# Seven products of half tiles in place of eight, in the output product of groups two to six

## The chip, the cores and the metric

The kernel runs on one NeuronCore of a Trainium2 chip. The metric is the device time of one execution in microseconds; where several runs were timed, their median.

## The reference

A gated linear attention runs over 4 batches, 8 heads, 768 steps and head size 48; its output, put together over the heads, goes through a feed-forward layer with a squared ReLU.

```python
for t in range(S):
    state = alpha[:, :, t, :, None] * state + np.einsum('bhd,bhe->bhde', k[:, :, t], v[:, :, t])
    y[:, :, t] = np.einsum('bhd,bhde->bhe', q[:, :, t], state)
...
x = np.ascontiguousarray(attn_out.transpose(0, 2, 1, 3)).reshape(B * S, H * D)
...
h = np.maximum(x @ w_in, 0.0)
return (h * h @ w_out).astype(np.float32)
```

x is 3072 x 384, w_in 384 x 2048, w_out 2048 x 384. The weights come as float64, everything else as float32.

## The kernel before, in words

The sequence is cut into chunks of 128 steps. One chunk of one batch is a block, so there are 24 blocks, four (the four batches of one chunk) to a group, and six groups. Each block goes through four stages of attention (line 402). Stage 1: aT turns alpha on TensorE, ln takes logarithms on ScalarE, sn sums them along the chunk on VectorE, eb and ei make the exponentials on ScalarE. Stage 2: qT and kT turn q and k, mq and mk scale them on VectorE into qs and ks. Stage 3: sc multiplies ks and qs, am masks the result on VectorE, kr turns ks back and kc copies it. Stage 4: kv makes the state's increment, sm and st update the state on VectorE, y makes the output, and ev copies it on ScalarE, in 12 pieces a block, into xT, the transposed input of the feed-forward layer.

The feed-forward layer works on a whole group of 512 rows. ffn_in (line 365) makes one of 16 hidden tiles of 128 x 512: three matmul calls of 512 columns, a ReLU on ScalarE into r, a square into hid, in group one on ScalarE and later on VectorE. ffn_out (line 381) is the output product: for each of four blocks t of the group, 16 calls of 384 columns are summed in one PSUM bank, 64 calls a group. ScalarE copies the bank out, and SP stores it. The weights stay in on-chip memory from group one on; there they are converted from float64, one of 16 pieces a slot (convert_first, convert_second).

The order is written out by hand: every engine works through its own queue in the program's order. The first blocks follow a list of steps (line 407). After that each group has 16 slots, one for each stage of each block of the next group (line 420). A slot emits its stage, one piece of weights, in the first slot of a block the loads of the block after, and then as many units of this group's feed-forward layer as its share of the columns allows. So the first eight slots hold two ffn_in units each, and the last eight hold four ffn_out units each. The last group has no attention beside it.

Buffers: three input tiles each for alpha, q and k, and four for v (NIN and NV, line 74); two of most work tiles (line 204); 16 hidden tiles; four PSUM banks for the feed-forward layer (ps_ffn) and four for attention. All loads and stores go through the queue of SP, in order, and a load waits there until its tile has been read.

Of the kernel before, what the change touches and what calls it, by code (L numbers as in the profile page):

```python
# [8 lines left out]
FP32 = mybir.dt.float32  # L9
U32 = mybir.dt.uint32  # L10
AF = mybir.ActivationFunctionType
ALU = mybir.AluOpType
# [3 lines left out]
GB = 4  # L16
# [7 lines left out]
def kernel(  # L24
# [22 lines left out]
    nc = tc.nc  # L47
    B, H, S, D = q.shape
    C = 128
    NCH = S // C  # L50
    NP = H // 2
    NBLK = B * NCH
    DM, DF = moe_w_in.shape
    KM = DM // 128
    NJ = DF // 128
# [4 lines left out]
    consts = ctx.enter_context(tc.tile_pool(name="consts", bufs=1))  # L60
    raw_pool = ctx.enter_context(tc.tile_pool(name="raw", bufs=NR))
    cv_pool = ctx.enter_context(tc.tile_pool(name="cv", bufs=2))
    hid_pool = ctx.enter_context(tc.tile_pool(name="hid", bufs=NJ))
    p2 = ctx.enter_context(tc.tile_pool(name="p2", bufs=2))
    x_pool = ctx.enter_context(tc.tile_pool(name="x", bufs=2))
    ps_att = ctx.enter_context(tc.tile_pool(name="ps_att", bufs=4, space=PSUM))
    ps_ffn = ctx.enter_context(tc.tile_pool(name="ps_ffn", bufs=GB, space=PSUM))
# [3 lines left out]
    def kept(name, n, shape):  # L71
        return [consts.tile(shape, FP32, name=f"{name}{i}") for i in range(n)]

    NIN = 3
    NV = 4
    tiles = {x: kept(f"{x}_in", NIN, [128, H, 64]) for x in "aqk"}
    for i in range(NIN):
        for x, value in (("a", 1.0), ("q", 0.0), ("k", 0.0)):
            nc.gpsimd.memset(tiles[x][i][:, :, D:64], value)
    tiles["v"] = kept("v_in", NV, [128, H * D])  # L80
    s_t = kept("s", B, [128, NP, 128])
# [6 lines left out]
    def load(n, xs="aqkv"):  # L88
        c, b = divmod(n, B)
        for x in xs:  # L90
            t = tiles[x][n % len(tiles[x])]
            nc.sync.dma_start(
                out=t.rearrange("a (h d) -> a h d", h=H) if x == "v" else t[:, :, 0:D],
                in_=srcs[x][b, :, c * C : (c + 1) * C, :].rearrange("h s d -> s h d"),
            )

    NW = 8
    w_in = [consts.tile([128, KM, DF // NW], FP32, name=f"w_in{i}") for i in range(NW)]
    w_out = [consts.tile([128, NJ // NW, DM], FP32, name=f"w_out{i}") for i in range(NW)]
    raws = {}  # L100

    def load_weights(i):
        dst = (w_in + w_out)[i]
        dt = moe_w_in.dtype
        raw = dst if dt == FP32 else raw_pool.tile(list(dst.shape), dt, tag="raw", name="raw")
        raws[i] = raw
        if i < NW:
            src = moe_w_in[:, i * DF // NW : (i + 1) * DF // NW]
            nc.sync.dma_start(out=raw, in_=src.rearrange("(k r) f -> r k f", r=128))
        else:  # L110
            i -= NW
            src = moe_w_out[i * DF // NW : (i + 1) * DF // NW, :]
            nc.sync.dma_start(out=raw, in_=src.rearrange("(j r) m -> r j m", r=128))
# [29 lines left out]
    def convert_second(i):  # L143
        if moe_w_in.dtype == FP32:
            return
        w, hi, power, upper = half.pop(i)
        nc.vector.scalar_tensor_tensor(  # L147
            out=power, in0=hi, scalar=0x80000000, in1=power,
            op0=ALU.bitwise_and, op1=ALU.bitwise_or,
        )  # L150
        nc.vector.scalar_tensor_tensor(
            out=w, in0=upper, scalar=2.0**-20, in1=w, op0=ALU.mult, op1=ALU.add
        )
        nc.vector.tensor_tensor(out=w, in0=w, in1=power.bitcast(FP32), op=ALU.mult)  # L154

    for n, xs in ((0, "aqk"), (1, "aqk"), (2, "a"), (0, "v"), (2, "qk")):
        load(n, xs)
    to_load = list(range(2 * NW))
    stage = [2]
# [1 line left out]
    def next_weights():  # L161
        i = stage[0]
        stage[0] += 1
        if to_load:
            load_weights(to_load.pop(0))
        if i <= 2 * NW:
            convert_second(i - 1)
        if i < 2 * NW:
            convert_first(i)
# [18 lines left out]
    for _ in range(2):  # L188
        nc.tensor.matmul(
            out=ps_att.tile([128, NP, C], FP32, tag="att", name="warm"),  # L190
            lhsT=am_t[0][:, 0, 0, :], rhs=am_t[0][:, 0], start=True, stop=True,
# [3 lines left out]
    blk = [{} for _ in range(NBLK)]  # L195
# [5 lines left out]
            return ps_ffn.tile([128, *shape], FP32, tag="f", name=name)  # L201
        return ps_att.tile([128, *shape], FP32, tag="att", name=name)

    def work(name, bufs=2):
        return p2.tile([128, NP, C], FP32, tag=name, name=name, bufs=bufs)

    def turned(x, n):
        rows = tiles[x][n % NIN].rearrange("a h d -> a (h d)")
        ps = blk[n][f"{x}T"] = bank(n, f"{x}T")
# [70 lines left out]

    def kc(n):
        if n // B < NCH - 1:
            t = blk[n]["kc"] = work("kc")
            nc.scalar.activation(out=t, in_=blk[n].pop("kr"), func=AF.Copy)  # L284

    def kv(n):
        if n // B < NCH - 1:
            ps = blk[n]["kv"] = bank(n, "kv", (NP, 2 * D))
            for p in range(NP):
                nc.tensor.matmul(  # L290
                    out=ps[:, p, :], lhsT=blk[n]["kc"][:, p, :],
                    rhs=tiles["v"][n % NV][:, 2 * p * D : 2 * (p + 1) * D], start=True, stop=True,
                )
# [4 lines left out]

    def sm(n):
        if n // B in range(1, NCH - 1):  # L300
            ps, t = blk[n]["kv"], p2.tile([128, NP, 2 * D], FP32, tag="sm", name="sm")
            for e in range(2):
                rows, s = state(n, e)
                cols = slice(e * D, (e + 1) * D)
                nc.vector.tensor_tensor(  # L305
                    out=t[rows, :, cols], in0=ps[rows, :, cols], in1=s, op=ALU.add
                )
            blk[n]["kv"] = t

    def y(n):  # L310
        v_in = tiles["v"][n % NV]

# [47 lines left out]
        blk[n].clear()  # L360


    hid, acc = {}, {}

    def ffn_in(g, j):
        hid[j] = hid_pool.tile([128, GB * C], FP32, tag="hid", name="hid")
        w, c0 = w_in[j * NW // NJ], j % (NJ // NW) * 128
        ps = ps_ffn.tile([128, GB * C], FP32, tag="f", name="h")
        for kk in range(KM):
            nc.tensor.matmul(  # L370
                out=ps, lhsT=w[:, kk, c0 : c0 + 128], rhs=xT[g][:, kk, :],
                start=(kk == 0), stop=(kk == KM - 1),
            )
        r = p2.tile([128, GB * C], FP32, tag="r", name="r")
        nc.scalar.activation(out=r, in_=ps, func=AF.Relu)  # L375
        if g == 0:
            nc.scalar.activation(out=hid[j], in_=r, func=AF.Square)  # L377
        else:
            nc.vector.tensor_tensor(out=hid[j], in0=r, in1=r, op=ALU.mult)  # L379

    def ffn_out(g, t, i):
        per = NJ // NW
        if i == 0:
            acc[t] = ps_ffn.tile([128, GB * C], FP32, tag="f", name="o")
        for j in range(per * i, per * (i + 1)):
            nc.tensor.matmul(  # L386
                out=acc[t][:, 0:DM],
                lhsT=hid[j][:, t * C : (t + 1) * C],
                rhs=w_out[i][:, j % per, :],
                start=(j == 0), stop=(j == NJ - 1),  # L390
            )
        if i == NW - 1:
            o = p2.tile([128, DM], FP32, tag="osb", name="osb")
            nc.scalar.activation(out=o, in_=acc.pop(t)[:, 0:DM], func=AF.Copy)  # L394
            c, b = divmod(g * GB + t, B)
            r0 = (b * NCH + c) * C
            nc.sync.dma_start(out=out[r0 : r0 + C, :], in_=o)

# [4 lines left out]
    steps["weights"] = lambda: load_weights(to_load.pop(0))  # L405
    steps["first"], steps["second"] = convert_first, convert_second
    first = """
        aT0 ln0 sn0 qT0 eb0 kT0 ei0 mq0 mk0 aT1 kr0 ln1 sc0 load3a load1v load3q load3k load2v
        weights load3v weights sn1 kc0 qT1 am0 eb1 kT1 ei1 mk1 load4a weights load4q load4k weights
        aT2 mq1 kr1 ln2 sc1 kc1 sn2 y0 am1 ei2 kv0 eb2 ev0 qT2 st0 kT2 load4v mq2 aT3 mk2 kr2 ln3  # L410
        sc2 kc2 sn3 kv1 am2 ei3 y1 eb3 kT3 ev1 st1 qT3 mk3 y2 mq3 sc3 ev2 kv2 am3 kr3 first0 y3
        st2 kc3 ev3 second0 kv3 first1 st3
    """
    for word in first.split():
        f = next(x for x in steps if word.startswith(x))
# [2 lines left out]

    NS = GB * len(stages)
    for g in range(NBLK // GB):  # L420
        units = [(ffn_in, (g, j)) for j in range(NJ)]

        outs = [(g, t, i) for t in range(GB) for i in range(NW)]
        units += [(ffn_out, a) for a in (outs if g else sorted(outs, key=lambda a: a[2]))]
        cost = {ffn_in: KM * GB * C, ffn_out: NJ // NW * DM}
        total = sum(cost[f] for f, _ in units)
        done = 0
        for slot in range(NS):
            i, s = divmod(slot, len(stages))
            n = (g + 1) * GB + i  # L430
            if n < NBLK:
                for f in stages[s]:
                    f(n)
            next_weights()
            if s == 0 and n + 1 < NBLK:
                load(n + 1)
            while units and done * NS < total * (slot + 1):
                f, args = units.pop(0)
                f(*args)
                done += cost[f]  # L440
# [30 lines left out]
```

## Time and profile before

| | |
|---|---|
| three runs | 654.16, 656.03 and 657.51 us, median 656.03 |
| the profiled execution | 653.49 us |
| its span, first to last instruction | 651.5 us |
| granted TensorE clock, mean | 0.994 |
| busy: TensorE, weight loads, VectorE, ScalarE | 638.5, 375.4, 233.3, 230.1 us |
| DMA | 36.63 MB, 56 GB/s over the span |

Engines are named as in the profile: PE is TensorE and PEld its weight loads, DVE is VectorE, ACT is ScalarE, SP issues the DMAs. A row of the costliest groups gives line, engine, operation, output and inputs, shape and count; then busy time in us and the mean of one in ns; then the idle time of the engine ahead of them and what ended it. Matmul records overlap, since each counts its own drain, so a mean is longer than the distance between two of them. The chain of waits is followed back from the last instruction to whatever released each step.

### The profile page before, as it was taken

To read this page: it belongs to the slowest core of one execution; us is meant where nothing else is said; L and a number is where in the kernel's file an instruction comes from. 1 tells how busy PE (TensorE), PEld (TensorE's weight loads), DVE (VectorE), ACT (ScalarE), POOL (GpSimd) and SP (SyncE) were. 2 spreads that over 40 slices of the span, in tenths; PEclk is the share of its full clock that TensorE was granted. 3 is DMA by queue.
4 is the path that set the end of the run, shared out by engine and by line. 5 is a ranking of instruction groups with operands and counts; after the bars stand their busy time and mean duration, and the time that the engine had idled before them with its cause. 6 is when DMAs were issued, how large, how long until landed. Compare 5 with 4: busy or idle time off the path is not lost.

```text
span 651.5 us, 7054 instructions
## 1 busy us (share of the span) xinstructions
PE 638.5 (98%) x2804; PEld 375.4 (58%) x2804; DVE 233.3 (36%) x363; ACT 230.1 (35%) x543; POOL 4.3 (1%) x21
## 2 busy tenths in 40 slices
PE   7799999999999999999999999999999999999997
PEld 4655456665556665555666555566655566544554
DVE  6686868734432113343211434221324211022100
ACT  4868674533432303434032342321332412222100
POOL 2000000000000000000000000000000000000000
PEclk9979999999999999999999999999999999999999
DMA  9985566009000124500030900003560000000000
GB/s 156 264 195 139 125 143 182 10 26 169 1 0 13 25 49 83 75 1 0 13 61 13 158 0 2 0 24 62 79 79 0 1 12 22 16 1 0 6 19 24
DMA packets 108704, 36.63 MB, mean 56 GB/s; under 512 B 100480, under 2 KB 103552, under 8 KB 108672
## 3 DMA queue, kind: packets, MB, share of 16 engines
q1 hardware_dynamic: 108672, 36.18, 30.0%
q8 instruction: 22, 0.36, 0.2%
q14 instruction: 10, 0.08, 0.1%
HBM read 31.46 MB, written 4.72 MB: 56 GB/s over the span
## 4 chain that ended last, share of the span: by engine, by line
PE 90%; ACT 5%; DVE 4%; issue 1%; DVEq 0%; ACTq 0%
PE o L386 38%; PE h L370 35%; PE sc L261 4%; PE y L325 3%; PE y L318 3%; PE kv L290 2%; ACT xT L345 2%; PE kr L279 2%; PE qT L211 1%; PE aT L211 1%; PE kT L211 1%; ACT hid L377 1%; ACT power L137 1%; DVE power L147 1%; ACT r L375 1%
## 5 line engine op out<-in xcount | busy, mean ns | idle before, releaser
L370 PE MATMUL h<-xT,w_in 128*128 128x512 f32 x576 | 257.1, 598 | 0.7 <-DVE w_in L154 0.7
L386 PE MATMUL o<-w_out,hid 128*128 128x384 f32 x768 | 255.8, 488 | 0.3 <-DVE w_out L154 0.3
L386 PEld LDWEIGHTS o<-w_out,hid 128*128 128x128 f32 x768 | 142.7, 190 | 93.8 <-issue 1.8
L370 PEld LDWEIGHTS h<-xT,w_in 128*128 128x128 f32 x576 | 106.9, 191 | 122.7 <-issue 119.9
L379 DVE TENSOR_TENSOR hid<-r 128x512 f32<-128x512 f32 x80 | 55.4, 692 | 170.4 <-ACT r L375 170.4
L345 ACT COPY xT<-y 32x128 f32<-32x128 f32 (+3 forms) x282 | 72.7, 258 | 90.9 <-PE y L325 86.1
L375 ACT ACTIVATE r<-h 128x512 f32<-128x512 f32 x96 | 57.0, 593 | 127.9 <-PE h L370 127.6
L225 DVE TENSOR_TENSOR_SCAN la<-again,la 128x512 f32<-128x512 f32 x24 | 29.3, 1221 | 77.3 <-ACT la L220 77.3
L394 ACT ACTIVATE osb<-o 128x384 f32<-128x384 f32 x24 | 11.7, 491 | 122.0 <-PE o L386 120.3
L269 DVE COPY_PREDICATED am<-causal,sc 128x512 f32<-128x512 uint32 x48 | 32.3, 728 | 49.5 <-PE sc L261 49.3
L261 PEld LDWEIGHTS sc<-qs,ks 48*128 48x128 f32 x384 | 23.3, 187 | 13.8 <-issue 10.8
L261 PE MATMUL sc<-qs,ks 48*128 48x128 f32 x384 | 27.9, 285 | 0.0
L325 PE MATMUL y<-am,v_in 128*48 128x128 f32 (+1 forms) x384 | 26.5, 278 | 1.4 <-ACT xT L345 1.4
L248 DVE TENSOR_TENSOR qs<-qT,b 128x512 f32<-128x512 f32 x24 | 16.6, 690 | 31.1 <-PE qT L211 30.0
L290 PEld LDWEIGHTS kv<-v_in,kc 128*128 128x128 f32 x160 | 21.5, 198 | 8.3 <-issue 4.0
L305 DVE TENSOR_TENSOR sm<-kv,s 48x192 f32<-48x192 f32 x32 | 11.3, 354 | 39.5 <-PE kv L290 39.0
L234 ACT ACTIVATE b<-la 128x512 f32<-128x512 f32 x24 | 15.1, 628 | 28.0 <-DVE la L225 28.0
L137 ACT ACTIVATE power<-power,rebias 128x768 uint32<-128x768 uint32 x16 | 15.0, 936 | 25.4 <-DVE power L130 25.3
L290 PE MATMUL kv<-v_in,kc 128*128 128x96 f32 x160 | 21.9, 281 | 1.7 <-ACT kc L284 1.7
L325 PEld LDWEIGHTS y<-am,v_in 128*48 128x48 f32 (+1 forms) x384 | 20.4, 129 | 4.6 <-ACT xT L345 1.8
L318 PE MATMUL y<-qs,s 128*128 128x128 f32 x160 | 21.6, 278 | 0.0
L318 PEld LDWEIGHTS y<-qs,s 128*128 128x128 f32 x160 | 19.8, 192 | 1.5 <-issue 1.0
(44 smaller groups left out, 274.9 us busy)
## 6 DMA issues: line engine op xcount, KB each, us to landing
raw<-in_moe_w_in_dram SPq DMA_DIRECT2D x8, 768.0 KB, 5.8
raw<-in_moe_w_out_dram SPq DMA_DIRECT2D x8, 768.0 KB, 4.4
a_in<-in_alpha_dram SPq DMA_DIRECT2D x24, 192.0 KB, 4.8
q_in<-in_q_dram SPq DMA_DIRECT2D x24, 192.0 KB, 5.0
k_in<-in_k_dram SPq DMA_DIRECT2D x24, 192.0 KB, 5.1
v_in<-in_v_dram SPq DMA_DIRECT2D x24, 192.0 KB, 4.9
out_dram<-osb SPq DMA_DIRECT2D x24, 192.0 KB, 1.9
```

Of the source, the lines that this page charges most:

```text
L137: nc.scalar.activation(out=power, in_=power, func=AF.Relu, scale=2.0**23, bias=rebias)
L225: nc.vector.tensor_tensor_scan(out=la.rearrange("a p t -> a (p t)"), data0=again.rearrange("a p t -> a (p t)"), data1=la.rearrange("a p t ...
L261: nc.tensor.matmul(out=ps[e][:, p, :], lhsT=blk[n]["ks"][rows, p, :], rhs=blk[n]["qs"][rows, p, :], start=True, stop=True,)
L269: nc.vector.copy_predicated(out=am_t[n % NAM][:, e], mask=causal.bitcast(U32).unsqueeze(1).to_broadcast([128, NP, C]), data=ps,)
L290: nc.tensor.matmul(out=ps[:, p, :], lhsT=blk[n]["kc"][:, p, :], rhs=tiles["v"][n % NV][:, 2 * p * D : 2 * (p + 1) * D], start=True, stop=True,
L318: nc.tensor.matmul(out=ys[p // per][:, p % per, :], lhsT=s_t[n % B][:, p, :], rhs=blk[n]["qs"][:, p, :], start=(p % per == 0), stop=False, ...
L325: nc.tensor.matmul(out=ys[p // per][64 * e : 64 * e + D + G * e, p % per, :], lhsT=v_in[:, (2 * p + e) * D - G * e : (2 * p + e + 1) * D], ...
L345: copy(out=xT[g][to : to + m, kk, t * C : (t + 1) * C], in_=ys[p // per][r : r + m, p % per, :],)
L370: nc.tensor.matmul(out=ps, lhsT=w[:, kk, c0 : c0 + 128], rhs=xT[g][:, kk, :], start=(kk == 0), stop=(kk == KM - 1),)
L375: nc.scalar.activation(out=r, in_=ps, func=AF.Relu)
L379: nc.vector.tensor_tensor(out=hid[j], in0=r, in1=r, op=ALU.mult)
L386: nc.tensor.matmul(out=acc[t][:, 0:DM], lhsT=hid[j][:, t * C : (t + 1) * C], rhs=w_out[i][:, j % per, :], start=(j == 0), stop=(j == NJ - 1),)
```

## The change

In groups two to six the output product is made by Strassen's algorithm. The hidden tiles of a group, as the matrix A, are halved along the rows of the group (256 each) and along the hidden dimension (tiles 0 to 7 and 8 to 15); w_out, as B, is halved along the hidden dimension and along its columns (192 each). In place of eight products of halves there are seven, of sums of halves, each of 4 r x 2 j x 2 t = 16 calls of 192 columns; ffn_product makes one r of one product. VectorE makes the sums: sum_hidden four per r and group, from the hidden tiles, three into a new tile s124 and one in place; sum_weights four per r once, in the first four slots of group two, three into new tiles t1, t2 and t4 and one in place of a quarter of w_out. The seven products go into four PSUM banks; products 2, 3 and 4 are added in PSUM to banks that hold 1, 5 and 7. VectorE adds the intermediate sums u1, u2 and u3 to the banks on the way out, ScalarE copies where nothing is added. The four stores of a group come after products 4 and 3, two each.

The order of ffn_in changes in these groups (tiles of the two halves in turn); the four sums of an r follow every fourth ffn_in. Slots get shares of the new number of columns. Input tiles go to two (three for v), most work tiles to one, and output and u tiles take over buffers of the weights' conversion. In the first section the loads move in the hand-written list to places behind the steps that free their tiles. Group one keeps its output product.

```diff
@@ -60,7 +60,7 @@
-    hid_pool = ctx.enter_context(tc.tile_pool(name="hid", bufs=NJ))
+    hid_pool = ctx.enter_context(tc.tile_pool(name="hid", bufs=NJ // 2))
@@ -71,8 +71,8 @@
-    NIN = 3
-    NV = 4
+    NIN = 2
+    NV = 3
@@ -153,7 +153,7 @@
-    for n, xs in ((0, "aqk"), (1, "aqk"), (2, "a"), (0, "v"), (2, "qk")):
+    for n, xs in ((0, "aqk"), (1, "aqk")):
@@ -201,7 +201,7 @@
-    def work(name, bufs=2):
+    def work(name, bufs=1):
@@ -280,7 +280,7 @@
-            t = blk[n]["kc"] = work("kc")
+            t = blk[n]["kc"] = work("kc", 2)
@@ -298,7 +298,7 @@
-            ps, t = blk[n]["kv"], p2.tile([128, NP, 2 * D], FP32, tag="sm", name="sm")
+            ps, t = blk[n]["kv"], p2.tile([128, NP, 2 * D], FP32, tag="sm", name="sm", bufs=1)
@@ -360,10 +360,39 @@
         blk[n].clear()
-    hid, acc = {}, {}
+    hid, acc, sums = {}, {}, {}
+    HT, HM, NR2 = GB * C // 2, DM // 2, NJ // 4
+    t1, t2, t4 = (kept(f"t{i}_", NR2, [128, 2, HM]) for i in (1, 2, 4))
+    def sum_weights(r):
+        b11, b12 = w_out[r][:, :, 0:HM], w_out[r][:, :, HM:DM]
+        b21, b22 = w_out[NR2 + r][:, :, 0:HM], w_out[NR2 + r][:, :, HM:DM]
+        for o, x, z in ((t1, b12, b11), (t2, b22, t1), (t4, b21, t2), (None, b22, b12)):
+            nc.vector.tensor_tensor(
+                out=o[r] if o else b12, in0=x, in1=z if not isinstance(z, list) else z[r],
+                op=ALU.subtract,
+            )
+    def halves(j):
+        return hid[j][:, :, 0:HT], hid[j][:, :, HT : 2 * HT]
+    def sum_hidden(r):
+        a11, a21 = halves(r)
+        a12, a22 = halves(NR2 + r)
+        s124 = raw_pool.tile([128, 3, 2, HT], FP32, tag="raw", name="s124")
+        s1, s2, s4 = sums[r] = s124[:, 0], s124[:, 1], s124[:, 2]
+        for o, x, op, z in (
+            (s1, a21, ALU.add, a22), (s2, s1, ALU.subtract, a11),
+            (a21, a11, ALU.subtract, a21), (s4, a12, ALU.subtract, s2),
+        ):
+            nc.vector.tensor_tensor(out=o, in0=x, in1=z, op=op)
     def ffn_in(g, j):
-        hid[j] = hid_pool.tile([128, GB * C], FP32, tag="hid", name="hid")
+        if j % 2 == 0:
+            hid[j // 2] = hid_pool.tile([128, 2, GB * C], FP32, tag="hid", name="hid")
         w, c0 = w_in[j * NW // NJ], j % (NJ // NW) * 128
         ps = ps_ffn.tile([128, GB * C], FP32, tag="f", name="h")
         for kk in range(KM):
@@ -373,28 +402,84 @@
             )
         r = p2.tile([128, GB * C], FP32, tag="r", name="r")
         nc.scalar.activation(out=r, in_=ps, func=AF.Relu)
+        h = hid[j // 2][:, j % 2, :]
         if g == 0:
-            nc.scalar.activation(out=hid[j], in_=r, func=AF.Square)
+            nc.scalar.activation(out=h, in_=r, func=AF.Square)
         else:
-            nc.vector.tensor_tensor(out=hid[j], in0=r, in1=r, op=ALU.mult)
+            nc.vector.tensor_tensor(out=h, in0=r, in1=r, op=ALU.mult)
+            if j >= NJ // 2 and j % 2:
+                sum_hidden(j // 2 - NR2)
+    def store(g, t, o):
+        c, b = divmod(g * GB + t, B)
+        r0 = (b * NCH + c) * C
+        nc.sync.dma_start(out=out[r0 : r0 + C, :], in_=o)
     def ffn_out(g, t, i):
         per = NJ // NW
         if i == 0:
             acc[t] = ps_ffn.tile([128, GB * C], FP32, tag="f", name="o")
-        for j in range(per * i, per * (i + 1)):
+        for j in range(per):
             nc.tensor.matmul(
                 out=acc[t][:, 0:DM],
-                lhsT=hid[j][:, t * C : (t + 1) * C],
-                rhs=w_out[i][:, j % per, :],
-                start=(j == 0), stop=(j == NJ - 1),
+                lhsT=hid[i][:, j, t * C : (t + 1) * C],
+                rhs=w_out[i][:, j, :],
+                start=(i == 0 and j == 0), stop=(i == NW - 1 and j == per - 1),
             )
         if i == NW - 1:
-            o = p2.tile([128, DM], FP32, tag="osb", name="osb")
+            if t % 2 == 0:
+                acc["out", t // 2] = cv_pool.tile([128, 2, DM], FP32, tag="upper", name="osb")
+            o = acc["out", t // 2][:, t % 2, :]
             nc.scalar.activation(out=o, in_=acc.pop(t)[:, 0:DM], func=AF.Copy)
-            c, b = divmod(g * GB + t, B)
-            r0 = (b * NCH + c) * C
-            nc.sync.dma_start(out=out[r0 : r0 + C, :], in_=o)
+            store(g, t, o)
+    PRODUCTS = (("1", 0), ("6", 1), ("2", 0), ("7", 2), ("5", 3), ("4", 2), ("3", 3))
+    def ffn_product(g, i, r):
+        name, k = PRODUCTS[i]
+        first = name in "1675"
+        if r == 0 and first:
+            acc[k] = ps_ffn.tile([128, 2, HM], FP32, tag="f", name="o")
+        (a11, s3), (a12, a22) = halves(r), halves(NR2 + r)
+        s1, s2, s4 = sums[r]
+        b11, t3 = w_out[r][:, :, 0:HM], w_out[r][:, :, HM:DM]
+        b21, b22 = w_out[NR2 + r][:, :, 0:HM], w_out[NR2 + r][:, :, HM:DM]
+        lhs, rhs = {
+            "1": (a11, b11), "2": (a12, b21), "3": (s4, b22), "4": (a22, t4[r]),
+            "5": (s1, t1[r]), "6": (s2, t2[r]), "7": (s3, t3),
+        }[name]
+        for j in range(2):
+            for t in range(2):
+                nc.tensor.matmul(
+                    out=acc[k][:, t, :], lhsT=lhs[:, j, t * C : (t + 1) * C], rhs=rhs[:, j, :],
+                    start=(first and r + j + t == 0), stop=(r == NR2 - 1 and j == 1),
+                    skip_group_check=True,
+                )
+        if r < NR2 - 1:
+            return
+        if name == "1":
+            for h in range(2):
+                acc["out", h] = cv_pool.tile([128, 2, DM], FP32, tag="upper", name="osb")
+            us = cv_pool.tile([128, 2, 2, HM], FP32, tag="power", name="us")
+            acc["u1"], acc["u2"] = us[:, 0], us[:, 1]
+            nc.scalar.activation(out=acc["u1"], in_=acc[k], func=AF.Copy)
+        elif name in "67":
+            u, new = ("u1", "u2") if name == "6" else ("u2", "u3")
+            if new == "u3":
+                acc[new] = p2.tile([128, 2, HM], FP32, tag=new, name=new, bufs=1)
+            nc.vector.tensor_tensor(out=acc[new], in0=acc[k], in1=acc[u], op=ALU.add)
+        else:
+            h, m, u = {"2": (0, 0, None), "5": (1, 1, "u3"), "4": (1, 0, "u2"), "3": (0, 1, "u2")}[name]
+            o = acc["out", h][:, :, m * HM : (m + 1) * HM]
+            if u:
+                nc.vector.tensor_tensor(out=o, in0=acc[k], in1=acc[u], op=ALU.add)
+            else:
+                nc.scalar.activation(out=o, in_=acc[k], func=AF.Copy)
+            if name in "43":
+                for t in range(2):
+                    store(g, 2 * h + t, acc["out", h][:, t, :])
@@ -405,11 +490,11 @@
...
-        aT0 ln0 sn0 qT0 eb0 kT0 ei0 mq0 mk0 aT1 kr0 ln1 sc0 load3a load1v load3q load3k load2v
+        aT0 load2a load0v ln0 sn0 qT0 load2q eb0 kT0 load2k ei0 mq0 mk0 aT1 load3a load1v kr0 ln1 sc0
...
@@ -418,11 +503,15 @@
     NS = GB * len(stages)
     for g in range(NBLK // GB):
-        units = [(ffn_in, (g, j)) for j in range(NJ)]
-        outs = [(g, t, i) for t in range(GB) for i in range(NW)]
-        units += [(ffn_out, a) for a in (outs if g else sorted(outs, key=lambda a: a[2]))]
-        cost = {ffn_in: KM * GB * C, ffn_out: NJ // NW * DM}
+        if g:
+            order = [j for r in range(NR2) for i in (r, NR2 + r) for j in (2 * i, 2 * i + 1)]
+            units = [(ffn_in, (g, j)) for j in order]
+            units += [(ffn_product, (g, i, r)) for i in range(len(PRODUCTS)) for r in range(NR2)]
+        else:
+            units = [(ffn_in, (g, j)) for j in range(NJ)]
+            units += [(ffn_out, (g, t, i)) for i in range(NW) for t in range(GB)]
+        cost = {ffn_in: KM * GB * C, ffn_out: NJ // NW * DM, ffn_product: 4 * HM}
         total = sum(cost[f] for f, _ in units)
         done = 0
         for slot in range(NS):
@@ -432,6 +521,8 @@
+            if g == 1 and slot < NR2:
+                sum_weights(slot)
```

TensorE, second slot of the second half of group two, before: the transposes of q and k, then four output units of two calls (o; a row per piece of w_out), then the next stage's sc.

```order
L211 MATMUL qT<-ident,q_in_85 128x128 x4
L211 MATMUL kT<-ident,k_in_88 128x128 x4
L386 MATMUL o<-w_out_123,hid 128x384 x2
L386 MATMUL o<-w_out_124,hid 128x384 x2
L386 MATMUL o<-w_out_125,hid 128x384 x2
L386 MATMUL o<-w_out_126,hid 128x384 x2
L261 MATMUL sc<-qs,ks 128x128 x8
```

The same slot now: two units of product 1 and two of product 6 (t_0 and t_1 are sums of weights, s_ sums of hidden halves).

```order
L211 MATMUL qT<-ident,q_in_83 128x128 x4
L211 MATMUL kT<-ident,k_in_85 128x128 x4
L455 MATMUL o<-w_out_114,hid 128x192 x4
L455 MATMUL o<-w_out_115,hid 128x192 x4
L455 MATMUL o<-t_0_154,s_1249 128x192 x4
L455 MATMUL o<-t_1_155,s_1347 128x192 x4
L261 MATMUL sc<-qs,ks 128x128 x8
```

Eight calls of 384 columns stood between kT and sc; sixteen of 192 stand there now, as many columns.

VectorE, from the fourth to the sixth slot of group three, before: the state's update (sm, s), the squares of two hidden tiles, the scan (la) of the next block, two squares, and the scaled q and k.

```order
L305 TENSOR_TENSOR sm<-kv,s_103 48x4x48 x2
L356 TENSOR_TENSOR s_103<-sm,b 48x4x48 x2
L379 TENSOR_TENSOR hid<-r 128x512 x2
L225 SCALAR_TENSOR_TENSOR la<-again,la 128x512
L379 TENSOR_TENSOR hid<-r 128x512 x2
L248 TENSOR_TENSOR qs<-qT,b 128x512
L248 TENSOR_TENSOR ks<-kT,inv 128x512
```

The same place now, with the four sums of hidden halves.

```order
L305 TENSOR_TENSOR sm<-kv,s_96 48x4x48 x2
L356 TENSOR_TENSOR s_96<-sm,b 48x4x48 x2
L409 TENSOR_TENSOR hid<-r 128x512 x2
L391 TENSOR_TENSOR s_1955<-hid 128x512
L391 TENSOR_TENSOR s_1955<-s_1955,hid 128x512
L391 TENSOR_TENSOR hid<-hid 128x2x256
L391 TENSOR_TENSOR s_1955<-hid,s_1955 128x512
L225 SCALAR_TENSOR_TENSOR la<-again,la 128x512
L409 TENSOR_TENSOR hid<-r 128x512 x2
L248 TENSOR_TENSOR qs<-qT,b 128x512
L248 TENSOR_TENSOR ks<-kT,inv 128x512
```

The scan of the next block, and with it that block's exponentials and scaled q and k, now stand behind four more instructions.

More of the change, by code (lines that the diff above doesn't have):

```diff
@@ L407 @@
     first = """
-        aT0 ln0 sn0 qT0 eb0 kT0 ei0 mq0 mk0 aT1 kr0 ln1 sc0 load3a load1v load3q load3k load2v
[L409 to L412, printed above, removed]
+        aT0 load2a load0v ln0 sn0 qT0 load2q eb0 kT0 load2k ei0 mq0 mk0 aT1 load3a load1v kr0 ln1 sc0
+        sn1 kc0 qT1 load3q am0 eb1 kT1 load3k load2v weights ei1 mk1
+        aT2 mq1 kr1 ln2 sc1 kc1 sn2 y0 am1 ei2 kv0 load3v weights load4a weights eb2 ev0 qT2 load4q
+        st0 kT2 load4k weights mq2 aT3 mk2 kr2 ln3 sc2 kc2 sn3 kv1 am2 ei3 y1 load4v eb3 kT3 ev1 st1
+        qT3 mk3 y2 mq3 sc3 ev2 kv2 am3 kr3 first0 y3 st2 kc3 ev3 second0 kv3 first1 st3
     """
```

## The prediction

> **What bounds the kernel now.** I read the page first: who is busy, then the chain that ended last.
>
> ```profile
> span 651.5 us, 7054 instructions
> PE 638.5 (98%) x2804; PEld 375.4 (58%) x2804; DVE 233.3 (36%) x363; ACT 230.1 (35%) x543; POOL 4.3 (1%) x21
> ...
> PEclk9979999999999999999999999999999999999999
> ...
> PE 90%; ACT 5%; DVE 4%; issue 1%; DVEq 0%; ACTq 0%
> PE o L386 38%; PE h L370 35%; PE sc L261 4%; PE y L325 3%; PE y L318 3%; PE kv L290 2%; ACT xT L345 2%; PE kr L279 2%; PE qT L211 1%; PE aT L211 1%; PE kT L211 1%; ACT hid L377 1%; ACT power L137 1%; DVE power L147 1%; ACT r L375 1%
> ...
> L370 PE MATMUL h<-xT,w_in 128*128 128x512 f32 x576 | 257.1, 598 | 0.7 <-DVE w_in L154 0.7
> L386 PE MATMUL o<-w_out,hid 128*128 128x384 f32 x768 | 255.8, 488 | 0.3 <-DVE w_out L154 0.3
> L386 PEld LDWEIGHTS o<-w_out,hid 128*128 128x128 f32 x768 | 142.7, 190 | 93.8 <-issue 1.8
> ```
>
> TensorE is busy 98% of the span, and L386, the output product that the change rewrites, is the largest piece of the chain. A busy TensorE can still be a waiting one, so the next view is the busy time of stretches; its first columns are the stretch, its length and PE's busy time.
>
> ```profile
> 0.00:40.00 40.00, 30.89 (x238) 22.59 (x239) 27.93 (x48) 25.45 (x65) 4.27 (x21) 0.91 1.15 209
> 40.00:140.00 100.00, 99.39 (x457) 59.20 (x456) 73.28 (x108) 60.13 (x113) 0.00 (x0) 1.00 0.48 114
> 340.00:440.00 100.00, 100.00 (x456) 59.25 (x455) 30.33 (x50) 31.57 (x82) 0.00 (x0) 1.00 0.21 32
> 440.00:540.00 100.00, 100.00 (x435) 57.88 (x434) 26.27 (x40) 29.90 (x79) 0.00 (x0) 1.00 0.26 38
> ```
>
> From 40 us on there is no hole in PE, while DVE (third busy column) works 26 to 30 us of a hundred in the groups that change. So from there the time is TensorE's records, one behind another, and I need their pace, not the mean of 488 ns, which counts the drain that the next record overlaps. The chain of waits in order of time gives it (start, duration, what).
>
> ```profile
> 456.18 0.86 PE kv L290 x8
> 457.05 0.92 PE y L318 x8
> ...
> 501.28 1.09 PE sc L261 x16
> ...
> 565.69 41.20 PE h L370 x96
> 606.89 41.30 PE o L386 x128
> ```
>
> The last group has no attention beside it: 16 tiles by 3 calls are 96 records, 64 output calls are 128. So each float32 matmul call is two records. Pace: 41.20/96 = 429.2 ns at 512 columns, 41.30/128 = 322.7 ns at 384. The line through both has 0.832 ns a column and 3 ns fixed. Weight loads are inside these paces.
>
> **The main term.** Per group of the last five, 64 calls of 384 columns become 7 products x 4 r x 2 j x 2 t = 112 calls of 192 columns: 128 records become 224, and the streamed columns fall by an eighth. A 192-column record is not in the trace. The line gives 322.7 - 192 x 0.832 = 163.0 ns. From below, half of 322.7 is 161.4. From above there are two rows: L318, 128 columns with the same full 128x128 weights, runs at 0.92/8 = 115.0 where the line has 109.7, so 5.3 ns over it, which would make 168.3; and the LDWEIGHTS record of 190 ns, were it the pace. I take 163: L290 with 96 columns and such weights goes at 0.86/8 = 107.5 ns, where the line has 82.8. There the load is the bound, and it is about 107 ns a record, well under 163; the 190 is a latency that overlaps. Sum: 128 x 322.7 = 41.30 us before, 224 x 163.0 = 36.51 after, 4.8 us a group, 24.0 us for five. Ends: 25.8 us gained (161.4), 18.0 (168.3), 6.3 lost (190). Break-even is 41.30/224 = 184 ns.
>
> The Trainium skill, in "TensorE: Matmul & The Clock Gate", section "Part 3: Packing small matmuls", says that a weight load overlaps running matmuls only when it goes to another row group. All these loads take all 128 rows, so by that rule doubling the loads would cost more than the columns save. The row against it is the 322.7 ns: it leaves 3 ns beside the columns, no room for a load of 107.
>
> **What VectorE gets.** It is added to an engine with room; what counts is who waits.
>
> ```profile
> L379 DVE TENSOR_TENSOR hid<-r 128x512 f32<-128x512 f32 x80 | 55.4, 692 | 170.4 <-ACT r L375 170.4
> L154 DVE TENSOR_TENSOR w_out<-w_out,power 128x768 f32<-128x768 f32 x8 | 7.7, 958 | 0.3
> L248 DVE TENSOR_TENSOR qs<-qT,b 128x512 f32<-128x512 f32 x24 | 16.6, 690 | 31.1 <-PE qT L211 30.0
> L305 DVE TENSOR_TENSOR sm<-kv,s 48x192 f32<-48x192 f32 x32 | 11.3, 354 | 39.5 <-PE kv L290 39.0
> ```
>
> Sums of hidden halves: 4 instructions x 4 r x 5 groups of 512 elements, 80 x 0.692 = 55.4 us. Weight sums: 16 of 384 elements, between the 692 and 958 rows carried down, 0.56 us each, 9 us. Combining products: 25 of 384 elements out of PSUM, between 354 and 690, 0.56 each, 14 us. DVE goes from 233 to about 312 us of some 630, half. ScalarE loses 10 of its output copies net.
>
> The four sums of one r (2.8 us) stand in DVE's queue after every fourth ffn_in. The worst place is the end of slot 3: behind the sums wait sn, then ScalarE's eb and ei, then the relus, squares, mq, mk, and TensorE's sc. This is that place in the timeline of before.
>
> ```profile
> 490.33 0.69 DVE L379 TENSOR_TENSOR hid<-r 128x512 f32<-128x512 f32 x1 [1.35 <-ACT r L375]
> 490.94 1.22 DVE L225 TENSOR_TENSOR_SCAN la<-again,la 128x512 f32<-128x512 f32 x1
> 492.19 0.63 ACT L234 ACTIVATE b<-la 128x512 f32<-128x512 f32 x1 [1.41 <-DVE la L225]
> 492.73 0.61 ACT L238 ACTIVATE inv<-la 128x512 f32<-128x512 f32 x1
> 493.25 0.58 ACT L375 ACTIVATE r<-h 128x512 f32<-128x512 f32 x1
> 493.86 0.69 DVE L379 TENSOR_TENSOR hid<-r 128x512 f32<-128x512 f32 x1 [1.70 <-ACT r L375]
> 497.13 0.68 DVE L248 TENSOR_TENSOR ks<-kT,inv 128x512 f32<-128x512 f32 x1
> ```
>
> With 2.8 us put in after 490.33 the scan starts at 493.7, the first relu at 496.05, the second at 496.65, the squares end at 498.0, ks ends at 499.3 instead of 497.8. The sc that needs it stands at 501.28 above: 2.0 us of cover remain, so nothing. The cover is gone if a sum takes over (2.0 + 2.8)/4 = 1.2 us. Weight sums (2.2 us a slot, slots 0 to 3 of group two) go behind sn, sm and mk, in slots where the cover is that or more; nothing. Combining adds read products that TensorE has finished by then; the attention steps queued behind them need later TensorE work anyway; nothing.
>
> **Handovers.** Slots 11 and 15 of a group get three product units, 24 records or 3.9 us, where 16 records of 5.2 us stood. Slot 11 of the last group with attention beside it shows the pattern.
>
> ```profile
> 534.91 5.43 PE L386 MATMUL o<-w_out,hid 128*128 128x384 f32 x16
> 535.02 3.29 ACT L345 COPY xT<-y 32x128 f32<-32x128 f32 x12 [7.87 <-PE y L325]
> 540.17 0.60 PE L211 MATMUL aT<-ident,a_in 128*128 128x128 f32 x4
> ```
>
> In slot 15 the same copies of y into xT are what the next group's ffn_in needs. In these times they are done at 538.3, and TensorE gets to ffn_in at 534.9 + 0.1 + 3.9 + 0.4 (aT) = 539.3. Covered by 1 us: nothing.
>
> **Fewer input buffers.** The DMA order on SP is unchanged in the first section, so only waits for buffers come in. The first is the third a_in, now behind aT of block 0.
>
> ```profile
> 5.33 0.60 PE L211 MATMUL aT<-ident,a_in 128*128 128x128 f32 x4
> ...
> 5.90 1.15 SPq L92 DMA_DIRECT2D a_in<-in_alpha_dram  x1
> ...
> 11.54 0.66 PE L211 MATMUL qT<-ident,q_in 128*128 128x128 f32 x4
> ...
> 12.92 1.09 SPq L92 DMA_DIRECT2D q_in<-in_q_dram  x1
> ```
>
> aT is over at 5.93, the load went at 5.90: 0.1 us later, with v, q, k behind it. The next such pair has qT over at 12.2, before its load at 12.92. I take 0.1 us (0 to 0.6). Later a load goes in the first slot of a block and is wanted four slots, over 20 us, on. The work tiles cut to one buffer are each read by TensorE or ScalarE before TensorE's own order reaches the next writer's input: nothing.
>
> **The end.** Before, one copy and one store follow the last matmul.
>
> ```profile
> 648.26 0.49 ACT L394 ACTIVATE osb<-o 128x384 f32<-128x384 f32 x1 [9.83 <-PE o L386]
> 648.77 0.33 SPq L397 DMA_DIRECT2D out_dram<-osb  x1
> ```
>
> After, an add of 0.56 and two stores, the second some 0.4 us behind: 0.5 us more. Sum: -24.0 + 0.1 + 0.5 = -23.4 on the profiled execution's 653.49 us, 630.1. The median of the runs shown, 656.03, is 1.0039 of that execution, so 632.5.
>
> **The rivals.**
> 1. VectorE's queue becomes a wait. For it: 2.0 us is thin, and I worked one place by hand. Against: the sums have the shape of L379. A stall of half a sum block, 1.4 us, in each of the four groups with attention beside them gives 5.6 us: 638.
> 2. The short record has L318's excess: 168.3 ns, 18.0 gained instead of 24.0: 638.5. For it the 115.0; against it L290's 107.5, which says that this excess is a load's pace showing, which at 163 has 50 ns of cover.
> 3. Slower: weight loads back to back at the recorded 190 ns set the pace, in the products alone. It decides from 184 ns on; 6.3 lost plus 0.6, 660.4, or 663 on the runs' scale. Against it L290's 107.5 between records whose loads are listed like these.
> 4. Load and stream one behind the other: 107.5 + 163 = 270 ns, 60.6 us a group where 41.3 stood, 96 lost: 753. The 322.7 speaks against it. This is what the Trainium skill's row-group rule in "TensorE: Matmul & The Clock Gate" would give.
> 5. The whole gain is eaten by waits (4.8 us a group): no change. Nothing in the rows makes so much.
>
> **How the numbers follow.** Forecast 0.76, its own range 630 to 636; rival 1 0.12, rival 2 0.06, rival 3 0.04, the fourth and fifth 0.01 each. The range begins at the forecast's lower bound, 1.8 us more gained, less some 2.5 for the spread of the runs (654.16 to 657.51 before), and ends 3 us above rivals 1 and 2: 628 to 641. A measurement of this kernel can tell about 0.5% from no change. Faster 0.94, same 0.01, slower 0.05.
>
> **What would show it.** Right: the last group's products read 36.5 us for 224 records in the chain, its h part 41.2 as now; PE stays at 100% in stretches from 40 us on; DVE about 310 us. Wrong: a pace of 168 or more (rivals 2 to 4); sc, L399 or the products waiting for DVE ks, sums or hid (rival 1); an aT waiting for a DMA (buffers).

## The result and the profile after

The changed kernel takes 631.97 us (median of four runs, 629.99 to 632.02); the kernel before took 656.0. The ratio is 0.963, with an interval of 0.960 to 0.966. The forecast was 632.5 us, between 628 and 641.

The page of the changed kernel, and its two rows of the feed-forward layer that compare with those of before (L399 is ffn_in, L455 a Strassen product; L455 is listed by the kind of its inputs, of which the largest is shown):

```profile
span 630.2 us, 8103 instructions
PE 616.5 (98%) x3284; PEld 438.9 (70%) x3284; DVE 305.3 (48%) x484; ACT 224.9 (36%) x533; POOL 3.8 (1%) x18
...
PE 89%; ACT 5%; DVE 4%; issue 1%; DVEq 0%
...
L399 PE MATMUL h<-xT,w_in 128*128 128x512 f32 x576 | 258.2, 599 | 1.5 <-DVE w_in L154 1.5
...
L455 PE MATMUL o<-w_out,hid 128*128 128x192 f32 x480 | 82.0, 327 | 0.0
```

TensorE is the bound as before, at 98%, now with 3284 records instead of 2804. VectorE has gone from 233 to 305 us and TensorE's products wait for none of it: the idle time ahead of L455 is 0.0, in this row and in its three others. The stretches (length, then PE's busy time, and further right DVE's) say the same.

```profile
40.00:140.00 100.00, 99.33 (x435) 57.99 (x434) 73.43 (x105) 60.47 (x112) 0.00 (x0) 0.99 0.51 118
...
240.00:340.00 100.00, 100.00 (x568) 74.10 (x567) 44.38 (x73) 31.66 (x82) 0.00 (x0) 1.00 0.24 40
440.00:540.00 100.00, 100.00 (x555) 74.10 (x554) 41.06 (x63) 29.86 (x79) 0.00 (x0) 1.00 0.19 32
```

Where the time came from is read off the chain of waits in order of time. First before, then after: the first ffn_in of group one, that of group two, and the last group.

```profile
35.76 7.11 PE h L370 x12
...
145.31 4.72 PE h L370 x11
```

```profile
37.76 7.60 PE h L399 x12
...
147.86 2.15 PE h L399 x5
...
548.74 41.20 PE h L399 x96
589.93 36.41 PE o L455 x224
```

The last ffn_in of before started at 565.69 and its last output product took 41.30. So from group two's start to the last group's it was 420.38 us before and is 400.88 now: 19.50 less for four groups, 4.88 each. The last group's products are 4.89 less. That is 24.4 us for five groups. Given back are 2.0 us by the first ffn_in, 0.55 more until group two, and 0.6 behind the last matmul (651.5 - 648.19 = 3.3 before, 630.2 - 626.34 = 3.9 now). The spans differ by 21.3 us accordingly. The 2.55 us of the beginning come from TensorE's clock and not from the change, as the experiments on the buffers and the holes show.

### The profile page after: what moved, and what is told of

It reads as the page before. It is cut to its first block, busy times and chain, and to the rows that moved or that the text cites. A ratio compares the mean times of both kernels' runs of the same rounds, so it can differ in the third digit from the quotient of the medians.

```text
span 630.2 us, 8103 instructions
## 1 busy us (share of the span) xinstructions
PE 616.5 (98%) x3284; PEld 438.9 (70%) x3284; DVE 305.3 (48%) x484; ACT 224.9 (36%) x533; POOL 3.8 (1%) x18
## 4 chain that ended last, share of the span: by engine, by line
PE 89%; ACT 5%; DVE 4%; issue 1%; DVEq 0%
PE h L399 36%; PE o L455 29%; PE o L423 6%; PE sc L261 4%; PE y L325 3%; PE y L318 3%; PE kv L290 2%; ACT xT L345 2%; PE kr L279 2%; PE qT L211 1%; PE aT L211 1%; PE kT L211 1%; ACT hid L407 1%; ACT power L137 1%; DVE power L147 1%
## 5 line engine op out<-in xcount | busy, mean ns | idle before, releaser
L399 PE MATMUL h<-xT,w_in 128*128 128x512 f32 x576 | 258.2, 599 | 1.5 <-DVE w_in L154 1.5
L399 PEld LDWEIGHTS h<-xT,w_in 128*128 128x128 f32 x576 | 106.7, 191 | 121.6 <-issue 119.3
L455 PE MATMUL o<-w_out,hid 128*128 128x192 f32 x480 | 82.0, 327 | 0.0
L455 PEld LDWEIGHTS o<-w_out,hid 128*128 128x128 f32 x480 | 78.1, 190 | 3.1 <-issue 3.1
L455 PE MATMUL o<-t,s 128*128 128x192 f32 x320 | 55.1, 326 | 0.0
L455 PEld LDWEIGHTS o<-t,s 128*128 128x128 f32 x320 | 52.1, 190 | 0.1
L423 PE MATMUL o<-w_out,hid 128*128 128x384 f32 x128 | 42.9, 489 | 0.3 <-DVE w_out L154 0.3
L423 PEld LDWEIGHTS o<-w_out,hid 128*128 128x128 f32 x128 | 23.7, 190 | 15.7 <-DVE w_out L154 0.5
L284 ACT ACTIVATE kc<-kr 128x512 f32<-128x512 f32 x20 | 11.9, 596 | 49.8 <-PE kr L279 49.8
L455 PE MATMUL o<-w_out,s 128*128 128x192 f32 x160 | 27.9, 329 | 0.0
L455 PE MATMUL o<-t,hid 128*128 128x192 f32 x160 | 27.6, 327 | 0.0
L455 PEld LDWEIGHTS o<-w_out,s 128*128 128x128 f32 x160 | 26.0, 190 | 0.7 <-issue 0.7
L455 PEld LDWEIGHTS o<-t,hid 128*128 128x128 f32 x160 | 26.0, 190 | 0.1
```

The lines of the kernel that those rows point to most:

```text
L399: nc.tensor.matmul(out=ps, lhsT=w[:, kk, c0 : c0 + 128], rhs=xT[g][:, kk, :], start=(kk == 0), stop=(kk == KM - 1),)
L423: nc.tensor.matmul(out=acc[t][:, 0:DM], lhsT=hid[i][:, j, t * C : (t + 1) * C], rhs=w_out[i][:, j, :], start=(i == 0 and j == 0), stop=(i ...
L455: nc.tensor.matmul(out=acc[k][:, t, :], lhsT=lhs[:, j, t * C : (t + 1) * C], rhs=rhs[:, j, :], start=(first and r + j + t == 0), stop=(r = ...
```

## The experiments

**A record of 192 columns by itself.** The kernel before, with each output call in groups two to six cut in two. Same columns, twice the records, no sums.

```diff
-            nc.tensor.matmul(
-                out=acc[t][:, 0:DM],
+        width = DM // 2 if g else DM
+            for c0 in range(0, DM, width):
+                nc.tensor.matmul(
+                    out=acc[t][:, c0 : c0 + width],
...
+                    rhs=w_out[i][:, j % per, c0 : c0 + width],
+                    start=(j == 0 and c0 == 0), stop=(j == NJ - 1),
```

> The kernel before with each output call of 384 columns in groups two to six split into two of 192: the same columns, twice the records and weight loads, no sums. Theory (a record of 192 columns takes its columns' time, 163 ns, its load hidden): 256 records x 163 = 41.7 us a group against 41.3, 2 us slower in all, 658. Rival of the load's recorded 190 ns: 48.6 us a group, 37 us slower, 693. Rival of load and stream one behind the other (270 ns): 69 us a group, 139 us slower, 795.

Measured: 657.55 us against 655.99 before, ratio 1.003 (1.000 to 1.005). The last group in the chain:

```profile
571.00 41.20 PE h L370 x96
612.20 41.61 PE o L388 x256
```

41.61/256 = 162.5 ns, and 0.31 us a group more than the 41.30 of uncut calls. Doubling the weight loads of 128 rows and columns cost nothing but 2.4 ns for each of the 128 more records. Both rivals, the 190 ns pace and the load ahead of each stream, are out by 35 us and more.

**Where the load's pace begins.** The same kernel with another width in each group.

```diff
-        width = DM // 2 if g else DM
+        width = (384, 192, 128, 96, 64, 192)[g]
```

> The kernel before, its output calls of 384 columns cut into pieces of another width in each group: 192 in group two, 128 in group three, 96 in four, 64 in five, 192 in six. Theory (a record takes the longer of its columns, 0.832 ns each and 3 ns, and of its weight load, about 112 ns when loads of 128 rows and columns follow each other): paces of 163, 112, 112, 112 and 163 ns; with 256, 384, 512, 768 and 256 records the output product of these groups takes 41.7, 43.0, 57.3, 86.0 and 41.7 us where it took 41.3, so 63 us more, 717 to 719. Rival (no such floor, the columns alone): 163, 110, 83, 56, 163 ns, each group's output within 2 us of 41.3, 5 us more in all.

Measured: 718.06 us, one run, against 654.49. One slot of each of the groups two to five in the chain, and the whole last one:

```profile
200.94 5.20 PE o L388 x32
...
307.76 5.36 PE o L388 x48
...
415.84 7.12 PE o L388 x64
...
535.48 10.67 PE o L388 x96
...
671.18 41.62 PE o L388 x256
```

Each time divided by its count gives 162.5 ns at 192 columns, 111.7 at 128, 111.3 at 96, 111.1 at 64, and 162.6 again at 192. From 64 to 128 columns a record with weights of 128 rows and columns costs 111 to 112 ns, whatever it streams; at 192 the columns bind, with 51 ns to spare. By the forecast's line of 0.832 ns a column and 3 ns the two meet at about 130 columns, which is an estimate, since no width between 128 and 192 ran. That the floor is the load's is argued and not shown by itself. It is at least no floor of every record: sc, whose weights take 48 rows, gets through 16 records of 128 columns in 1.16 us, at most 73 ns each. The forecast's main term rests on this, and a second halving, to 96 columns, would run at the floor.

**Without the sums.** The changed kernel, its products fed with plain halves; TensorE's work is as it was.

```diff
-        s124 = raw_pool.tile([128, 3, 2, HT], FP32, tag="raw", name="s124")
-        s1, s2, s4 = sums[r] = s124[:, 0], s124[:, 1], s124[:, 2]
...
-            nc.vector.tensor_tensor(out=o, in0=x, in1=z, op=op)
+        sums[r] = a21, a11, a12
```

(and sum_weights, t1, t2 and t4 left out likewise)

> The changed kernel without the sums of hidden halves and of weights: the seven products take plain halves, so the output is not the reference's; TensorE's records and the adds on the way out stay. Theory (VectorE's sums are wholly covered): 632 us, within 1 us of the changed kernel. Rival (some of the sums end in waits of TensorE): over 3 us faster, under 629.

Measured: 632.04 us (629.37 to 632.16), ratio to before 0.964 (0.960 to 0.967), as the changed kernel. DVE's busy time falls by 58 us, and from group two on the records stand at the same distances:

```profile
PE 617.4 (98%) x3284; PEld 440.0 (70%) x3284; DVE 247.2 (39%) x388; ACT 225.2 (36%) x533; POOL 3.8 (1%) x18
```

```profile
148.05 5.15 PE h L387 x12
...
548.91 41.20 PE h L387 x96
590.11 36.41 PE o L443 x224
```

400.86 us from group two to the last group, where the changed kernel has 400.88. VectorE's sums of halves cost nothing that can be seen. The adds on the way out are still in this run; for them the 0.0 us of idle time ahead of L455 speaks.

**The sums twice.** How thin the cover is.

```diff
             (a21, a11, ALU.subtract, a21), (s4, a12, ALU.subtract, s2),
-        ):
+        ) * 2:
```

> The changed kernel with the four sums of hidden halves made twice (the second set gives other values, so the output is not the reference's): 2.7 us more on VectorE behind every fourth ffn_in, 54 us more in all. Theory (the sums have a cover of 2.1 to 2.2 us ahead of sc in slots 6 and 10 of a group, and of 2.0 ahead of y in group five's first half): waits of some 0.6 + 0.5 us in each of four groups and 0.7 twice in one, 6 us, so 638. Rival (VectorE at 48% has room, so nothing): 632. Rival (waits pass on to the steps behind them and add up to the sums' whole 2.7 us at each of 16 places with attention beside them): 43 us, 675.

Measured: 634.18 us (633.97 to 637.8), ratio to before 0.969 (0.965 to 0.973). From group two to the last group:

```profile
145.34 5.15 PE h L399 x12
...
550.72 41.20 PE h L399 x96
591.92 36.41 PE o L455 x224
```

405.38 us, 4.50 more than the changed kernel: not nothing, and a tenth of what a wait of the whole length at 16 places would make. (The medians are only 2.2 us apart, because three of these four executions ran at a mean clock of 0.995 and three of the changed kernel's four at 0.991.) The place is the one forecast. In the changed kernel, slots 4 to 6 of a group, VectorE's rows and TensorE's sc:

```profile
377.92 0.69 DVE L409 TENSOR_TENSOR hid<-r 128x512 f32<-128x512 f32 x1 [1.34 <-ACT r L404]
378.65 0.69 DVE L391 TENSOR_TENSOR s<-hid 128x512 f32<-128x512 f32 x1
...
380.59 0.69 DVE L391 TENSOR_TENSOR s<-hid,s 128x512 f32<-128x512 f32 x1
381.19 1.22 DVE L225 TENSOR_TENSOR_SCAN la<-again,la 128x512 f32<-128x512 f32 x1
...
386.04 0.68 DVE L248 TENSOR_TENSOR ks<-kT,inv 128x512 f32<-128x512 f32 x1
```

```profile
388.80 1.16 PE L261 MATMUL sc<-qs,ks 48*128 48x128 f32 x16
```

ks is ready at 386.72 and sc runs at 388.80: 2.1 us of cover. With the sums twice, the same slots:

```profile
382.52 0.69 DVE L391 TENSOR_TENSOR s<-hid,s 128x512 f32<-128x512 f32 x1
...
387.98 0.68 DVE L248 TENSOR_TENSOR ks<-kT,inv 128x512 f32<-128x512 f32 x1
...
388.71 1.16 PE L261 MATMUL sc<-qs,ks 48*128 48x128 f32 x16 [0.43 <-DVE ks L248]
```

ks is ready at 388.66 and sc now waits for it. Of the 6 us expected, 4.5 came. Groups two to four lost 0.95 to 0.98 us each where 1.1 was expected. Most of what is missing is in group five, the last with attention beside it, which lost 1.61 where 2.5 was expected: y waited there once, for 0.17 us, instead of twice for 0.7. Why was not tried; a wait that lengthens one slot gives VectorE more time in the next, which would do it.

**The buffers alone.** The kernel before with two input tiles (three for v), single work tiles and the new places of the loads.

```diff
-    NIN = 3
-    NV = 4
+    NIN = 2
+    NV = 3
...
-    def work(name, bufs=2):
+    def work(name, bufs=1):
...
```

> The kernel before with the change's buffers and load places alone: two input tiles (three for v), one of most work tiles, the new places of the loads in the first section. Theory (loads have time to spare): 656 us, within 1 us of before; what the first section loses in the changed kernel, 2.0 us up to the first ffn_in, came from TensorE's clock and not from the loads. Rival (the loads, now behind the transposes that free their tiles, hold back the first section): 2 us slower, 658, with the first ffn_in 2 us later while the clock in the first 30 us is as before.

Measured: 655.38 us against 655.99, ratio 1.000 (0.998 to 1.002). The buffers cost nothing that can be measured here, which leaves room for 1.3 us. Its profiled execution (657.49 us) cannot tell the two explanations apart: its first ffn_in stands at 38.65, and its clock was half from 10.55 to 16.40. What moved the beginning by 2 us is seen by setting other traces side by side. The sums-twice kernel has the changed kernel's buffers, the split kernel those of before. First the fifth aT and the first ffn_in of sums-twice, then the early transposes of the split kernel:

```profile
34.39 1.06 PE L211 MATMUL aT<-ident,a_in 128*128 128x128 f32 x4
35.78 7.10 PE L399 MATMUL h<-xT,w_in 128*128 128x512 f32 x12 [0.33 <-DVE w_in L154]
```

```profile
13.61 1.11 PE L211 MATMUL qT<-ident,q_in 128*128 128x128 f32 x4
14.51 1.06 PE L211 MATMUL kT<-ident,k_in 128*128 128x128 f32 x4
```

With few buffers the first ffn_in stands at 35.78, as before the change (35.76). With all buffers four transposes took 1.1 us instead of 0.6, and the first ffn_in stood at 38.73. So the shift comes with the clock and goes without it, whichever buffers the kernel has.

The column behind the five engines is the granted clock; here are stretches of the changed kernel's profiled execution.

```profile
8.10:11.50 3.40, 1.55 (x16) 1.15 (x16) 2.70 (x4) 2.00 (x4) 0.00 (x0) 1.00 1.50 177
11.50:14.90 3.40, 3.40 (x26) 3.18 (x23) 1.47 (x3) 1.37 (x3) 0.00 (x0) 0.50 1.52 164
14.90:35.40 20.50, 16.25 (x179) 13.59 (x178) 15.35 (x29) 17.04 (x51) 0.00 (x0) 1.00 1.04 237
35.40:42.20 6.80, 5.73 (x13) 2.78 (x12) 5.53 (x9) 3.48 (x7) 0.00 (x0) 0.50 0.89 186
```

After a stretch in which TensorE worked 1.55 of 3.40 us it ran 3.4 us at half clock, and again 6.8 us around the first ffn_in. In the execution of before the first of these is missing; a stretch with 2.04 us of work did not bring it on, one with 0.66 was followed by the second:

```profile
8.50:11.90 3.40, 2.04 (x23) 1.75 (x24) 2.61 (x4) 2.34 (x5) 0.00 (x0) 1.00 1.50 178
29.00:32.40 3.40, 0.66 (x8) 0.42 (x8) 2.01 (x7) 3.28 (x8) 0.00 (x0) 1.00 1.21 252
...
5.10:32.40 27.30, 20.66 (x217) 16.82 (x215) 19.28 (x33) 19.95 (x54) 0.00 (x0) 1.00 1.28 226
32.40:39.20 6.80, 6.32 (x16) 3.99 (x17) 5.48 (x10) 3.97 (x10) 0.00 (x0) 0.50 0.89 212
```

By the kr behind the half clock of 11.50 to 14.90 (15.66 us, 13.69 before) the 2.0 us are complete, and 1.3 of them arise in that stretch. The other 0.7 is older: the changed kernel's first aT, at 5.56, takes 1.06 us where that of before took 0.60, and the first kr comes 0.69 us later. First before, then after:

```profile
9.86 0.66 PE L279 MATMUL kr<-ident,ks 128*128 128x128 f32 x4 [1.46 <-DVE ks L248]
```

```profile
5.56 1.06 PE L211 MATMUL aT<-ident,a_in 128*128 128x128 f32 x4
...
10.55 0.66 PE L279 MATMUL kr<-ident,ks 128*128 128x128 f32 x4 [1.85 <-DVE ks L248]
```

This slow start does not show in the clock column, which reads 1.00 from 4.70 to 8.10.

**Filling the holes.** To test the clock, the changed kernel got five calls of constants in holes of TensorE in the first section; their results are not read.

```diff
...
+            nc.tensor.matmul(
+                out=kept_bank["f"], lhsT=ident, rhs=again, start=True, stop=True,
+            )
...
```

> The changed kernel with five matmul calls of constants put into holes of TensorE in the first 36 us (one after the second aT, one between the halves of the fourth y, two behind it, one before the fifth aT); their results are not read. Theory (what differs in the first section from execution to execution, and the half clock around the first ffn_in, come from TensorE's clock falling in these holes): the clock stays full from its first rise, the first twelve records of ffn_in take 5.2 us instead of 7.1 to 7.6, 2 to 3 us less than the best execution of the changed kernel, so 627 to 629. Rival (the calls only stand in the way of the first section): 632 or more.

Measured: 630.18 us (630.14 to 630.24), the changed kernel beside it 631.92 (629.68 to 633.32), against 654.49 before. The mean clock is 0.999 to 1.000 in every execution, and the spread is gone, but the 627 to 629 us expected were missed: it was not under the best execution of the changed kernel. One call stood in the way: it waited for a bank and held the second half of a y.

```profile
28.76 0.66 PE L337 MATMUL y<-am,v_in 128*48 128x128 f32 x8
30.83 1.13 PE L204 MATMUL fill<-again,ident 128*128 128x512 f32 x2 [1.41 <-ACT xT L357]
31.88 0.66 PE L337 MATMUL y<-am,v_in 128*48 128x128 f32 x8
```

Beside it ran the changed kernel once more:

> The changed kernel again, beside the one with filled holes: 630 to 632, by the clock of its first section.

It gave 631.92, as above. Then the same without that call:

> The kernel with filled holes without its call between the halves of the fourth y, which there waited for a bank and put the second half from 30.2 to 31.9. Theory (that call cost what the full clock gained): the second half is back at 30.2, the first ffn_in at 35.8, the clock stays full; the second pair of ffn_in is then held by the conversion of its weights, at about 42.4 instead of 43.6, so about 1.1 us under the best execution of the changed kernel (629.7 to 630.0): 628.8, with little spread. Rival (the clock falls again without that call): 630 to 632, as the changed kernel.

And the changed kernel beside it:

> The changed kernel beside it: 630 to 633, by the clock of its first section.

Measured: the filled kernel without that call took 629.14 us (628.60 to 629.20), ratio to before 0.960 (0.957 to 0.962); the changed kernel had 629.93 (629.82 to 633.31), 0.962 (0.960 to 0.965). The first section of the filled kernel:

```profile
30.36 0.66 PE L335 MATMUL y<-am,v_in 128*48 128x128 f32 x8 [1.40 <-ACT xT L355]
30.95 1.98 PE L204 MATMUL fill<-again,ident 128*128 128x512 f32 x4
...
35.92 5.39 PE L409 MATMUL h<-xT,w_in 128*128 128x512 f32 x12 [0.73 <-DVE w_in L154]
...
42.65 2.84 PE L409 MATMUL h<-xT,w_in 128*128 128x512 f32 x6 [0.46 <-DVE w_in L154]
```

The first twelve records take 5.4 us instead of 7.6, and then the conversion of the weights holds the next ones. All five runs are below every run of the changed kernel in these measurements (lowest 629.68). The two ratios' intervals overlap, so a gain of 0.8 us in the median is not shown beyond the noise; that the spread is gone is.

## Why the prediction was right

**The main term** was 4.8 us a group, 24.0 in all, from 163.0 ns a record. The runs show 162.5 ns (36.41/224) and 4.88 us a group, 24.4 in all. The line through two paces of the trace gave the third to 0.3%. Its upper bounds did not come into play. Records of 128 columns with such weights go at 111.7 ns, 2.0 over the line's 109.7, so a part of L318's excess is the floor showing; its other 3.3 ns stay open. The floor is 111 ns and not the 107 taken from L290, which changes nothing at 163. The 190 ns of a load's record is a latency: records with a load each follow each other every 111 ns.

**VectorE's queue** was given 2.0 us of cover at sc; it is 2.1 in the group shown, and 2.2 in group five, where the forecast worked it out (ks ready at 486.93, sc at 489.13). The run without sums shows that nothing of the 58 us is on the path, the run with sums twice that 2.7 us more are too many for this cover. Rival 1 names a real place, which the change does not reach. The sums' own sizes were right, and VectorE's whole busy time came out at 305 us where 312 were forecast.

**The handovers and the buffers**: nothing and 0.1 us forecast; the buffers alone measure a ratio of 1.000, and in sums-twice, whose clock was as before, the third a_in goes at 5.96 us, 0.06 after the 5.90 of before. The four groups' distances leave no room for a wait between groups. **The end**: 0.5 us forecast, 0.6 measured.

**What the sum left out** is the first section's clock. The forecast took the beginning over from one execution of before, with its clock, and scaled by 1.0039 to the median. The change's own parts, -24.4 + 0.6, give 629.7 us on that execution's 653.49, and the execution of the changed kernel with a mean clock of 0.994, as that one had, took 629.99. The median of 631.97 belongs to executions at 0.991. So 632.5 was met with its scale factor doing the clock's part, without the forecast knowing what it stood for. That the median came within 0.5 us is luck: of the changed kernel's next two sets of executions, one has its median at 631.92 and the other at 629.93, with the same kernel.

The rules of the Trainium skill: in "TensorE: Matmul & The Clock Gate", "Part 3: Packing small matmuls", weight loads are said to overlap running matmuls only in another row group. All loads here take all 128 rows, and 162.5 ns for 192 columns with a load each disagrees. The same section names an exception, a load into a background weight buffer; rival 4 left it out, and these runs do not contradict it. In "Part 1: The HAM clock gate" of the same page, the clock is set to half or full by activity in free-running windows of 3413 ns, so that the same kernel differs from run to run; the stretches of 3.4 and 6.8 us at 0.50 agree.

## What to carry to other kernels

Where TensorE is busy without holes, count its records and take each one's distance to the next, not its duration. With weights of 128 rows and columns in float32 it was here the longer of the columns (0.83 ns each and 3 ns) and a floor of 111 ns, most likely the load of the next weights. Trading columns for more and shorter records pays in full as long as the shorter record outlasts that floor. What the other engines get in exchange is free only up to the cover of the step that TensorE waits for next, and that cover, 2 us here, is read in one place of the timeline, not from an engine's share of busy time.

## What the runs showed of the hardware

A hole in TensorE's work can cost twice: after a 3.4 us stretch with 1.55 us of work, the next 3.4 us ran at a clock of 0.50. Executions of one kernel differ in this: the changed kernel took 629.68 us at a mean clock of 0.994 and 633.32 at 0.989. Constant matmuls in the holes removed the spread (628.60 to 629.20, at 1.000); TensorE's first ffn_in and the next ones then waited for the conversion of the weights, 0.73 and 0.46 us.
